# Sine and cosine of a spatial gate: theta by channels on full tiles, products carried to tokens by DMA transposes

## The chip, the cores and the metric

One core of a Trainium2 chip runs the whole program in one launch. The metric is the device time of one execution in microseconds. TensorE (PE) does the matrix products, VectorE (DVE), ScalarE (ACT) and GpSimd (POOL) the elementwise work, SyncE (SP) issues all DMAs.

## What is computed

Three layers in a row, for 4 batches of 576 tokens and 512 channels: an attention (8 heads, half of them local, half strided), a gated layer, and the layer that the change is about. Cut to the latter, with `x` the output of the gated layer:

```python
def _moe2_ref(x, w_theta, w_tok_r, w_tok_i, w_ch):      # x: (4, 576, 512)
    theta = x @ w_theta
    cos_t, sin_t = (np.cos(theta), np.sin(theta))
    zr = x * cos_t
    zi = x * sin_t
    yr = np.einsum('ts,bsd->btd', w_tok_r, zr)           # mixes tokens
    yi = np.einsum('ts,bsd->btd', w_tok_i, zi)
    u = x + yr + yi
    return (u + np.maximum(u @ w_ch, 0.0)).astype(np.float32)
```

The kernel keeps every operand as two float16 numbers, a high part and the rest (a low part), and forms a product in three passes: high by high, low by high, high by low.

## The kernel before

The batches run one after the other, b = 0 to 3. Each has these stages on PE, named by the tile that the products go to:

- `v` (`main_v`), tokens on partitions: 48 matmuls of 512 columns, and 12 on the last 64 tokens; a layer norm on DVE and ACT turns it into `vn`.
- `u` and `sp` (`main_mid`): the two halves of the gate, channels on partitions, pairs of 288 columns.
- `x` (tiles `x20` to `x23`, four chunks of 128 channels): the gated layer's output. `x2_evac` (L622) copies it to `x2f` (float32), splits it into `x2h` (high and low), and issues two DMA transposes per chunk, high and low, each 128 x 640, that put the same numbers token-major into `zz`, a view of `zf`.
- `th` (L651 on): theta with tokens on partitions. Two pairs of full tiles of 128 tokens and one tile of the last 64, in `TH_ORDER` (0, 2, 1): 48 matmuls of 512 columns and 12 for the last 64 tokens, whose halves go to two halves of the array and are added by `fold_tail`. For each of the five token tiles (`ta`), on 512 channels: ACT rounds theta / 2 pi to an integer; DVE takes it off (`ta<-ta,th`) and clamps the rest (`ta<-ta`); ACT makes the absolute value, the cosine and the sine; POOL puts `x` together again from the transposed halves (`xt<-zf`); DVE multiplies twice (`ta<-ta,xt`); and each product is split into high (DVE or ACT) and low (DVE or POOL, `zf<-ta,zf`).
- `y` (`main_end`): the token mixing. `zz` has 9 slots of 128 rows (4 of cosine, 4 of sine, one with the last 64 tokens of both); each chunk of 128 channels takes 54 matmuls of 288 columns, that is 9 slots, 3 passes, 2 halves. Every chunk needs every slot. `TOK_GROUPS` lets chunks 0 and 1 start on slots 0 and 4 before the rest is there.
- `c`: the last product, and the output.

Around these run two things that have no stage of their own. `conv` turns the weights, which lie in memory as 64-bit floats, into float16 pairs (`tok_part` for the token weights), in batch 0. The attention of batch b + 1 runs in steps beside the stages of batch b (`sc`: scores; `sm`: softmax on DVE, ACT and POOL; `pT`: the transposed weights; `av`: the product with the values, which goes to `xT`, the input of `v`). When a step is written into the program is decided by a clock that counts PE columns: the stages are generators, and at every `yield` `others()` emits what is due.

After `main_mid(b)`, `drain(b + 1)` finishes the next batch's attention and `main_v(b + 1)` comes before `main_end(b)`; in batch 0 four steps of `main_end` (all of chunks 0 and 1) come ahead of that. So between `th` and `y` of one batch stands `v` of the next, but for the last batch, where `y` follows `th` directly.

All PE stages share three PSUM tiles `pm`; a stage waits until the tile three back is read. Each engine and each queue works in the order of its own list; a scheduler in the language makes the lists from the program, with the work of `hv`, `ha` and `hg` put ahead of other work.

Of the kernel before, what the change touches and what calls it, by code (L numbers as in the profile page):

```python
# [27 lines left out]
PI_IN = 3.1415925  # L28
# [39 lines left out]
def kernel(  # L68
# [175 lines left out]
    def tok_part(r, i):  # L244
        o = r * NF + i
        w = (w_tr, w_ti)[r]
        prep_w(wtok[:, 0, o, :], wtok[:, 1, o, :], w[i * P:(i + 1) * P, :], S)

    def tok_tail():
# [338 lines left out]
    def main_mid(b):  # L588
# [59 lines left out]

        for pr in TH_ORDER:
            rows = P if pr < 2 else TL  # L650
            nt = 2 if pr < 2 else 1  # L651
# [244 lines left out]
```

## Time and profile before

| what | us |
|---|---|
| median of 3 runs (557.25 to 558.96) | 557.27 |
| the profiled execution | 559.4 |
| its span, first to last instruction | 557.6 |
| PE busy in it | 488.9 |
| DVE busy in it | 402.2 |
| ACT busy in it | 314.8 |
| POOL busy in it | 178.0 |
| mean granted clock of TensorE | 0.969 of 2.4 GHz |

The busy time of an engine is what its instructions cover. The profile also gives, for each idle stretch of an engine, what ended it: `[2.60 <-POOL zf L110]` in the timeline says that the engine stood for 2.60 us until an instruction of POOL that writes `zf` was done. Line 110 is the helper through which all work of `hv`, `ha` and `hg` goes, L492 the matmul of a stage, L420, L389 and L456 the attention's. The granted clock of a stretch is 1.00 at 2.4 GHz and 0.50 at 1.2 GHz.

### The profile page before, as it was taken

To read this page: it belongs to the slowest core of one execution; us is meant where nothing else is said; L and a number is where in the kernel's file an instruction comes from. 1 tells how busy PE (TensorE), PEld (TensorE's weight loads), DVE (VectorE), ACT (ScalarE), POOL (GpSimd) and SP (SyncE) were. 2 spreads that over 40 slices of the span, in tenths; PEclk is the share of its full clock that TensorE was granted. 3 is DMA by queue.
4 is the path that set the end of the run, shared out by engine and by line. 5 is a ranking of instruction groups with operands and counts; after the bars stand their busy time and mean duration, and the time that the engine had idled before them with its cause. 6 is when DMAs were issued, how large, how long until landed. Compare 5 with 4: busy or idle time off the path is not lost. (4 is left out here: it accounts for less than half of the span.)

```text
span 557.6 us, 10326 instructions
## 1 busy us (share of the span) xinstructions
PE 488.9 (88%) x3836; PEld 346.6 (62%) x3836; DVE 402.2 (72%) x998; ACT 314.8 (56%) x767; POOL 178.0 (32%) x131
## 2 busy tenths in 40 slices
PE   5888969596788969998997979999989999998896
PEld 4664747474355647776644767777437777764575
DVE  2787889989999989889489958874499531228712
ACT  3776868576776467776457267765563212145401
POOL 0464245566564540002062320010252500106320
PEclk9889989989989998999999998999999999999899
DMA  7666665548125214875810016523400010050002
GB/s 277 198 228 242 210 213 190 162 121 177 36 73 165 69 40 95 214 165 136 170 21 0 1 30 160 153 39 65 69 0 1 1 59 29 1 95 2 1 0 86
DMA packets 59478, 55.69 MB, mean 100 GB/s; under 512 B 43554, under 2 KB 44578, under 8 KB 59428
## 3 DMA queue, kind: packets, MB, share of 16 engines
q1 hardware_dynamic: 59428, 55.04, 36.3%
q8 instruction: 30, 0.49, 0.4%
q14 instruction: 20, 0.16, 0.1%
HBM read 40.08 MB, written 4.72 MB: 80 GB/s over the span
## 5 line engine op out<-in xcount | busy, mean ns | idle before, releaser
L492 PE MATMUL y<-wtok,zf 128*128 128x288 f16 x864 | 111.3, 289 | 13.2 <-POOL zf L110 4.9
L492 PEld LDWEIGHTS <-zf 128*128 128x128 f16 x864 | 84.0, 99 | 40.1 <-POOL zf L110 6.0
L338 ACT ACTIVATE sm<-sm,st 96x128 f32<-96x128 f32 (+1 forms) x132 | 51.4, 391 | 14.5 <-DVE st L329 13.1
L492 PE MATMUL sp<-wsp,vn 128*128 128x288 f16 x384 | 51.6, 289 | 2.0 <-ACT vn L110 1.9
L492 PE MATMUL c<-x2h,wch 128*128 128x288 f16 x384 | 51.7, 296 | 0.7 <-ACT o L110 0.7
L492 PE MATMUL th<-wth,x2h 128*128 128x512 f16 (+1 forms) x240 | 52.0, 394 | 0.0
L492 PE MATMUL x<-zf,wout 128*128 128x288 f16 x384 | 51.1, 292 | 0.0
L110 POOL TENSOR_TENSOR x2h<-x2f,x2h 128x576 f16<-128x576 f32 x20 | 27.9, 1396 | 71.0 <-issue 37.6
L492 PE MATMUL u<-xT,win 128*128 128x288 f16 x384 | 49.3, 286 | 0.0
L492 PEld LDWEIGHTS <-vn 128*128 128x128 f16 x416 | 40.6, 99 | 13.0 <-ACT vn L110 2.2
L110 POOL TENSOR_TENSOR zf<-u,zf 128x576 f16<-128x576 f32 x8 | 11.1, 1392 | 114.9 <-ACT zf L110 114.9
L110 POOL TENSOR_TENSOR xt<-zf 128x512 f32<-128x512 f16 (+1 forms) x20 | 32.2, 1616 | 47.0 <-DMA zf<-x2h 24.4
L492 PEld LDWEIGHTS <-wch 128*128 128x128 f16 x384 | 38.5, 101 | 11.7 <-issue 0.9
L492 PEld LDWEIGHTS <-wout 128*128 128x128 f16 x384 | 37.6, 100 | 10.5 <-issue 0.4
L553 PE MATMUL v<-win,xT 128*128 128x512 f16 x192 | 43.8, 379 | 0.3 <-ACT xT L357 0.3
L492 PEld LDWEIGHTS <-win 128*128 128x128 f16 x384 | 37.3, 98 | 9.2
L492 PEld LDWEIGHTS <-x2h 128*128 128x128 f16 (+1 forms) x240 | 21.7, 103 | 26.3 <-issue 5.8
L329 DVE CUSTOM_DVE_ANT_0 sm<-sc,mask 96x128 f32<-96x128 f32 (+1 forms) x132 | 32.1, 280 | 3.4 <-PE av L420 2.0
L110 ACT ACTIVATE ta<-ta 128x512 f32<-128x512 f32 (+1 forms) x40 | 23.9, 618 | 17.9 <-DVE ta L110 17.8
L553 PEld LDWEIGHTS <-xT 128*128 128x128 f16 x192 | 18.6, 98 | 21.6 <-ACT xT L357 0.6
L110 POOL TENSOR_TENSOR zf<-ta,zf 128x512 f16<-128x512 f32 x16 | 23.3, 1456 | 18.8 <-ACT zf L110 18.8
L110 DVE TENSOR_TENSOR ta<-ta,xt 128x512 f32<-128x512 f32 x32 | 25.7, 836 | 3.9 <-ACT ta L110 3.9
(127 smaller groups left out, 941.8 us busy)
## 6 DMA issues: line engine op xcount, KB each, us to landing
qs<-in_qd_dram SPq DMA_DIRECT2D x16, 288.0 KB, 3.0
out_dram<-o SPq DMA_DIRECT2D x15, 288.0 KB, 2.6
x2f<-in_w_in_dram SPq DMA_DIRECT2D x8, 512.0 KB, 5.5
ks<-in_kl_dram SPq DMA_DIRECT2D x8, 304.0 KB, 3.2
k<-in_kzs_dram SPq DMA_DIRECT2D x4, 576.0 KB, 5.4
wstg<-in_w_tr_dram SPq DMA_DIRECT2D x4, 576.0 KB, 4.6
wstg<-in_w_ti_dram SPq DMA_DIRECT2D x4, 576.0 KB, 3.9
ks<-in_ks_dram SPq DMA_DIRECT2D x8, 288.0 KB, 3.5
```

The source lines that it names most:

```text
L110: return f(*args, **kwargs)
L329: nc.vector.tensor_tensor_reduce(out=sm[0:R, n, :], in0=sc[n][0:R], in1=mask[0:R, mi, :], op0=ALU.add, op1=ALU.min, scale=-0.125, scalar=3e38,
L338: nc.scalar.activation(sm[0:R, n, :], sm[0:R, n, :], AF.Exp, bias=st[0:R, 1, n:n + 1], scale=-1.0, accum_out=st[0:R, 2, n:n + 1])
L492: nc.tensor.matmul(ps, lhs, rhs, **kw)
L553: nc.tensor.matmul(ps, xh[:, xe, c, i * P:(i + 1) * P], win[:, we, c, DM:2 * DM], start=(c == 0 and n == 0), stop=(c == NC - 1 and n == 2))
```

## The change

Theta is computed with channels on partitions, like the stages around it. `th_mm` uses the weights as the stationary operand: four chunks of 128 channels, 24 matmuls of 288 columns each, no tile of 64 rows. `z_chunk` then works on 128 channels by 576 tokens: ACT rounds theta, now as a number of turns, to an integer; DVE forms the fraction in one step from PSUM (`TURNS` is the factor); the clamp is gone, since the sine is taken of `TURN`, a little under 2 pi, times the fraction; ACT makes absolute value, cosine and sine; DVE multiplies both halves by `x2f` in one instruction of 128 x 1152; `split` makes the high part on ACT and the low part on DVE, each 128 x 1152, into one of two buffers `zbs` that lie in `vn`. Two DMA transposes of 128 x 1152 per chunk carry them token-major into `zz`, nine blocks each: columns 0 to 575 of a buffer are cosine, 576 to 1151 sine, so the slots of `zz`, and with them the rows of `wtok`, run on without a gap. The transposes of `x2h`, the sums `xt`, and the padding of `x2h` fall away.

`main_end` takes the chunks one by one over all nine slots; a chunk needs only its own 128 channels of `zz`. Its first four steps in batch 0 no longer come ahead of `main_v(1)`.

```diff
-            for e in range(2):
-                nc.sync.dma_start_transpose(out=zz[:, 0:NF + 1, e, m * P:(m + 1) * P], in_=x2h[:, e, m, :])
...
-            for t in range(nt):
-                a = s2("ta")
...
-                ha.activation(ia, tv, AF.Copy, scale=1.0 / (PS * 2 * math.pi))
-                hv.scalar_tensor_tensor(bv, ia, -2 * math.pi * PS, tv, op0=ALU.mult, op1=ALU.add)
-                hv.tensor_scalar(bv, bv, PI_IN * PS, -PI_IN * PS, op0=ALU.min, op1=ALU.max)
-                ha.activation(av, bv, AF.Abs)
-                ha.activation(av, av, AF.Sin, bias=halfpi[r], scale=-1.0 / PS)
-                ha.activation(bv, bv, AF.Sin, scale=1.0 / PS)
-                o = 2 * pr + t
-                H[E_XADD[b > 0]].tensor_tensor(xv, zz[r, o, 0, :], zz[r, o, 1, :], ALU.add)
...
+        def z_chunk(m, ps):
+            a = s2(f"ta{m}")
+            flat = a.rearrange("p a n -> p (a n)")
+            turns, f = a.bitcast(I32)[:, 0, :], a[:, 1, :]
+            ha.activation(fold(turns), halves(ps), AF.Copy, scale=TURNS)
+            hv.scalar_tensor_tensor(fold(f), halves(ps), TURNS, fold(turns), op0=ALU.mult, op1=ALU.subtract)
+            ha.activation(a[:, 0, :], f, AF.Abs)
+            ha.activation(a[:, 0, :], a[:, 0, :], AF.Sin, bias=halfpi, scale=-TURN)
+            ha.activation(f, f, AF.Sin, scale=TURN)
+            hv.tensor_tensor(a, a, x2f[:, m, :].unsqueeze(1).broadcast_to([P, 2, S]), ALU.mult)
+            zb = zbs[m % 2]
+            split((zb[:, 0, :], zb[:, 1, :]), flat, H[E_ZLO[m + 4 * (b > 0)]])
+            for e in range(2):
+                nc.sync.dma_start_transpose(out=zz[:, :, e, m * P:(m + 1) * P], in_=zb[:, e, :])
...
+        for m in range(NC):
             ps = pm(f"y{m}")
-            tok_mm(ps, m, (0, 1, 4, 5, 2, 3, 6, 7, 8), True, True)
-            tok_evac(m, ps)
-            yield
+            for i in range(NZ):
+                for n, (ze, we) in enumerate(PASS):
+                    mm2(ps, zz[:, i, ze, m * P:(m + 1) * P], wtok[:, we, i, :],
+                        i == 0 and n == 0, i == NZ - 1 and n == 2)
+                if i == NZ - 1:
+                    tok_evac(m, ps)
+                if i % 3 == 2:
+                    yield
...
         if b + 1 < B:
-            for _ in range(4 if b == 0 else 0):
-                next(end, None)
-                others()
             drain(b + 1)
             run_main(main_v(b + 1))
```

The lists of the engines change with it. On DVE in the last batch, from its first instruction on `th`, before:

```order
L110 SCALAR_TENSOR_TENSOR ta_5568<-ta_5568,th0_5543 128x512
L110 TENSOR_SCALAR ta_5568<-ta_5568 128x512
L110 SCALAR_TENSOR_TENSOR ta_5583<-ta_5583,th0_5543 128x512
L110 TENSOR_SCALAR ta_5583<-ta_5583 128x512
L110 TENSOR_TENSOR ta_5568<-ta_5568,xt_5569 128x512 x2
L110 CAST zf_95<-ta_5568 128x512
L110 TENSOR_TENSOR zt_5611<-th2_5598,xt_5613 64x512
L110 TENSOR_TENSOR zf_95<-ta_5568,zf_95 128x512
L110 TENSOR_TENSOR ta_5583<-ta_5583,xt_5584 128x512 x2
L110 CAST zf_95<-ta_5583 128x512
L110 SCALAR_TENSOR_TENSOR ta_5612<-ta_5612,zt_5611 64x512
L110 TENSOR_TENSOR zf_95<-ta_5583,zf_95 128x512
```

These are two of the five token tiles and the start of the third; the list goes on in the same way for 14 more rows. The whole of this work in the same batch, now:

```order
L108 SCALAR_TENSOR_TENSOR ta0_5569<-th0_5525,ta0_5569 128x576
L108 SCALAR_TENSOR_TENSOR ta1_5586<-th1_5526,ta1_5586 128x576
L108 TENSOR_TENSOR ta0_5569<-ta0_5569,x2f_96 128x1152
L108 SCALAR_TENSOR_TENSOR ta2_5622<-th2_5597,ta2_5622 128x576
L108 TENSOR_TENSOR vn_94<-ta0_5569,vn_94 128x1152
L108 TENSOR_TENSOR ta1_5586<-ta1_5586,x2f_96 128x1152
L108 SCALAR_TENSOR_TENSOR ta3_5658<-th3_5633,ta3_5658 128x576
L108 TENSOR_TENSOR ta2_5622<-ta2_5622,x2f_96 128x1152
L108 TENSOR_TENSOR vn_94<-ta1_5586,vn_94 128x1152
L108 TENSOR_TENSOR vn_94<-ta2_5622,vn_94 128x1152
L108 TENSOR_TENSOR ta3_5658<-ta3_5658,x2f_96 128x1152
L108 TENSOR_TENSOR vn_94<-ta3_5658,vn_94 128x1152
```

Thirty instructions on DVE have become twelve, and none of them has 64 rows or reads what POOL wrote.

On ACT in batch 0, at the end of the next batch's attention (`pT32` is its last transposed softmax, `xT1_93` its output, the input of `v`), before:

```order
L110 ACTIVATE zf_95<-ta_1563 128x512
L421 ACTIVATE pT32_1464<-av_1536 128x512
L121 ACTIVATE kT_1838<-ks_1881 128x608
L121 ACTIVATE qT_1941<-qs_1943 128x576
L110 ACTIVATE ta_1592<-ta_1592 64x512
L110 ACTIVATE ta_1654<-th1_1607 128x512
L110 ACTIVATE ta_1592<-ta_1592,halfpi_76 64x512
L110 ACTIVATE ta_1592<-ta_1592 64x512
L110 ACTIVATE ta_1639<-ta_1639 128x512
L357 ACTIVATE xT1_93<-av_1617 128x18x14
```

and now:

```order
L108 ACTIVATE vn_94<-ta2_1611 128x1152
L108 ACTIVATE ta3_1654<-ta3_1654,halfpi_76 128x576
L108 ACTIVATE ta3_1654<-ta3_1654 128x576
L423 ACTIVATE pT32_1456<-av_1546 128x512
L119 ACTIVATE kT_1853<-ks_1904 128x608
L292 ACTIVATE vT_1910<-vs_1850 128x768
L108 ACTIVATE vn_94<-ta3_1654 128x1152
L359 ACTIVATE xT1_93<-av_1622 128x18x14
```

The attention's copy `pT32` stood in the middle of the sine work, after two of five tiles; it now stands behind the last sine of the last chunk, and the last `xT` behind the last high part.

On PE in batch 0, where `v` of batch 1 meets that (`sc_1952` is the first score of batch 2's attention), now:

```order
L494 MATMUL v2_1748<-win_78,xT1_93 64x512
L435 LDWEIGHTS qT_1852
L435 MATMUL sc_1952<-kT_1853,qT_1852 96x128
L435 LDWEIGHTS qT_1852
L435 MATMUL sc_1952<-kT_1853,qT_1852 96x128
L391 MATMUL av_1622<-pT32_1456,v32_1276 64x126 x4
L435 LDWEIGHTS qT_1852
L435 MATMUL sc_1952<-kT_1853,qT_1852 96x128
```

Before, the same `av` product (there `av_1617`) stood between matmuls of `y0` and `y1`. Those have moved behind `v`, and ahead of `av` now stand 21 of the 60 matmuls of `v`, the ones that don't need the last heads.

## Rows read from the trace of the kernel before

**Rows 1.** waits of TensorE: engine, line, releaser: us in total, times, longest us

```profile
PE sc L433 <- DVE st L329: 8.9, 6, 4.1
...
PE y L492 <- POOL zf L110: 4.9, 2, 2.6
...
PE y L492 <- ACT vr L110: 3.9, 4, 1.0
PE v L492 <- DVE ta L110: 3.6, 2, 1.9
```

**Rows 2.** timeline of TensorE, batch 3: start us, us, instructions [idle before <-releaser]

```profile
483.20 11.92 PE L492 MATMUL x<-zf,wout 128*128 128x288 f16 x96
494.96 12.04 PE L492 MATMUL th<-wth,x2h 128*128 128x512 f16 x60
506.84 1.34 PE L492 MATMUL y<-wtok,zf 128*128 128x288 f16 x8
510.78 5.01 PE L492 MATMUL y<-wtok,zf 128*128 128x288 f16 x38 [2.60 <-POOL zf L110]
517.82 1.03 PE L492 MATMUL y<-wtok,zf 128*128 128x288 f16 x7 [2.04 <-ACT zf L110]
519.35 21.80 PE L492 MATMUL y<-wtok,zf 128*128 128x288 f16 x163 [0.50 <-DVE zf L110]
```

**Rows 3.** timeline of TensorE, batch 1: v of batch 2, and a score inside c

```profile
284.14 10.52 PE L553 MATMUL v<-win,xT 128*128 128x512 f16 x48
...
333.76 0.61 PE L433 MATMUL sc<-kT,qT 128*96 128x128 f16 x8 [2.48 <-DVE st L329]
```

**Rows 4.** timeline of TensorE, batch 0: the end of y

```profile
208.05 0.61 PE L433 MATMUL sc<-kT,qT 128*96 128x128 f16 x8 [4.11 <-DVE st L329]
...
209.69 3.21 PE L492 MATMUL c<-x2h,wch 128*128 128x288 f16 x15
```

**Rows 5.** timeline of VectorE, batch 0: its first instruction on theta

```profile
148.09 0.67 DVE L110 SCALAR_TENSOR_TENSOR ta<-ta,th 128x512 f32<-128x512 int32 x1
```

**Rows 6.** stretches: us; busy us of PE, PEld, DVE, ACT, POOL; PEclk, DMA share, GB/s

```profile
157.60:209.60 52.00, 42.49 (x321) 28.09 (x319) 50.22 (x101) 30.71 (x59) 25.96 (x16) 0.99 0.28 80
```

**Rows 7.** groups by shape, all batches: busy us, mean ns of one, idle before

```profile
L110 DVE TENSOR_TENSOR ta<-ta,xt 128x512 f32<-128x512 f32 x32 | 25.7, 836 | 3.9 <-ACT ta L110 3.9
...
L110 ACT ACTIVATE ta<-ta 128x512 f32<-128x512 f32 x32 | 19.0, 617 | 0.1
...
L110 ACT ACTIVATE ta<-ta,halfpi 128x512 f32<-128x512 f32 x16 | 11.4, 715 | 0.2
...
L110 DVE SCALAR_TENSOR_TENSOR x2f<-y,x2f 128x576 f32<-128x576 f32 x16 | 12.1, 753 | 19.8 <-PE y L492 19.6
...
L110 ACT ACTIVATE x2f<-x 128x576 f32<-128x576 f32 x16 | 10.2, 646 | 12.8 <-PE x L492 12.7
...
L110 ACT ACTIVATE vn<-vr 128x1024 f16<-128x1024 f32 x8 | 8.1, 1043 | 0.2 <-DVE vr L110 0.2
...
L110 DVE TENSOR_TENSOR vn<-vr,vn 128x1024 f16<-128x1024 f32 x4 | 4.8, 1212 | 0.0
```

**Rows 8.** DMA issues by line: count, median us to landing

```profile
zf<-x2h SPq DMA_TRANSPOSE x32, 2.6
...
pT<-ph SPq DMA_TRANSPOSE x22, 3.1
```

**Rows 9.** instructions on zf from SyncE, all 32 transposes: landing

```profile
DMA to landing us min/median/max: 2.6/2.6/4.4
```

**Rows 10.** stretches as in rows 6: batch 3's eight transposes, then three after waits

```profile
486.00:508.00 22.00, 21.98 (x143) 12.95 (x140) 8.37 (x14) 12.05 (x20) 4.97 (x4) 1.00 0.35 61
111.00:116.00 5.00, 4.40 (x24) 2.90 (x25) 3.03 (x14) 3.42 (x12) 2.97 (x4) 0.50 0.09 14
334.00:338.00 4.00, 4.00 (x27) 2.76 (x25) 3.78 (x15) 3.48 (x16) 0.51 (x1) 0.63 0.30 80
518.00:524.00 6.00, 5.50 (x32) 3.61 (x31) 5.97 (x10) 3.55 (x7) 1.56 (x2) 0.72 0.00 0
```

More of the change, by code (lines that the diff above doesn't have):

```diff
@@ L27 @@
 SS = SPS * VNS
-PI_IN = 3.1415925
+TURN = 6.283185
+TURNS = 1.0 / (PS * 2 * math.pi)
 AHEAD = 200
@@ L153 @@
     zf = const.tile([P, (NF + 1) * 2 * DM + 2 * NC * S], F16, name="zf")
-    zz = zf[:, 0:(2 * NF + 1) * 2 * DM].rearrange("p (i e d) -> p i e d", i=2 * NF + 1, e=2)
+    zz = zf[:, 0:NZ * 2 * DM].rearrange("p (i e d) -> p i e d", i=NZ, e=2)
     gT = zf[:, (NF + 1) * 2 * DM:].rearrange("p (e c s) -> p e c s", e=2, c=NC)
+    zbs = [vn.rearrange("p i e d -> p (i e d)")[:, i * 4 * S:(i + 1) * 4 * S].rearrange("p (e n) -> p e n", e=2)
+           for i in range(2)]
     x2f = const.tile([P, NC, S], F32, name="x2f")
-    x2h = const.tile([P, 2, NC, (NF + 1) * P], F16, name="x2h")
+    x2h = const.tile([P, 2, NC, S], F16, name="x2h")
     def s2(name):
@@ L242, in sp_tail, with tok_part @@
                                        op0=ALU.mult, op1=ALU.subtract)
[L244 to L249, printed above, removed]
-        stg, x = stage()
-        for j, w in enumerate((w_tr, w_ti)):
-            nc.sync.dma_start(stg[j * TL:(j + 1) * TL, :], w[T0:S, :])
-        part(wtok[:, 0, 2 * NF, :], wtok[:, 1, 2 * NF, :], from_f64(stg, x, S), True)
+    def tok_part(i):
+        stg, x = stage()
+        r = 0
+        while r < P:
+            g = i * P + r
+            w, k = (w_tr, g) if g < S else (w_ti, g - S)
+            n = min(P - r, S - k)
+            nc.sync.dma_start(stg[r:r + n, 0:S], w[k:k + n, :])
+            r += n
+        part(wtok[:, 0, i, :], wtok[:, 1, i, :], from_f64(stg, x, S), True)
     SOFF = [0, 126, 252, 378, 448]
@@ new lines, in th_mm @@
+        def th_mm(m, ps, cs):
+            for c in cs:
+                for n, (we, xe) in enumerate(PASS):
+                    mm2(ps, wth[:, we, c, m * P:(m + 1) * P], x2h[:, xe, c, :],
+                        c == 0 and n == 0, c == NC - 1 and n == 2)
+        tiles = [pm(f"th{i}") for i in range(2)]
+        for cs in ((0, 1, 2), (3,)):
+            for m in range(2):
+                th_mm(m, tiles[m], cs)
+                if cs[0] == 3:
+                    z_chunk(m, tiles[m])
+                yield
@@ L692, in main_mid @@
+        for m in (2, 3):
+            ps = pm(f"th{m}")
+            th_mm(m, ps, range(NC))
+            z_chunk(m, ps)
             yield
     def main_end(b):
-        slot = list(range(NF)) + list(range(NF + 1, 2 * NF + 1)) + [NF]
-        def tok_mm(ps, m, tiles, first, last):
-            for i in tiles:
-                for n, (ze, we) in enumerate(PASS):
-                    mm2(ps, zz[:, slot[i], ze, m * P:(m + 1) * P], wtok[:, we, i, :],
-                        first and i == tiles[0] and n == 0, last and i == tiles[-1] and n == 2)
@@ L707, in tok_evac @@
             split((x2h[:, 0, m, 0:S], x2h[:, 1, m, 0:S]), x, H[E_YLO[m + 4 * (b > 0)]], E_YHI[m + 4 * (b > 0)])
-        tiles = [pm(f"y{i}") for i in range(2)]
-        for part, grp in enumerate(TOK_GROUPS):
-            end = part == len(TOK_GROUPS) - 1
-            for m in range(2):
-                tok_mm(tiles[m], m, grp, part == 0, end)
-                if end:
-                    tok_evac(m, tiles[m])
-                yield
-        for m in (2, 3):
-            ps = pm(f"y{m}")
-            tok_mm(ps, m, (0, 1, 4, 5, 2, 3, 6, 7, 8), True, True)
-            tok_evac(m, ps)
-            yield
+        for m in range(NC):
+            ps = pm(f"y{m}")
+            for i in range(NZ):
[6 more added lines that the diff above has]
+                    yield
         for m0 in (0, 2):
@@ L760 @@
     timed(list(sq_parts(wth, w_th)) + [switch], *CONV_TH)
-    timed([lambda r=r, i=i: tok_part(r, i) for i in range(NF) for r in range(2)] + [tok_tail], *CONV_TOK)
+    timed([lambda i=i: tok_part(i) for i in range(NZ)], *CONV_TOK)
     timed(sq_parts(wch, w_ch), *CONV_CH)
```

41 lines of the change are left out of this document (3 added, 38 removed).

## The prediction

> **What bounds the kernel now.** TensorE, stage by stage; so I read first what it waits for, then its timeline in each batch, then which engine is full there. Of the waits [rows 1], four kinds belong to the stretch from theta to the end of `y` and `c`: on POOL's and ACT's share of the products (`zf`), on ACT's `vr`, on DVE's `ta`, and on DVE's `st`, the scores of the attention that wait for the softmax before them. In batch 3 nothing stands between `th` and `y` [rows 2]: `y` starts at 506.84 on two of its nine slots, then waits 2.60, 2.04 and 0.50 us, 5.1 in all, for the rest of the products. In batches 1 and 2 `v` of the next batch lies between, and the products are not waited for; what is late there is a PSUM tile: the last part of `v` waits for a theta tile that DVE has not read, twice, 3.6 us together, and `y` four times for a tile that ACT has not emptied, 3.9 us [rows 1]. In batch 1 a score inside `c` then waits 2.48 us [rows 3], in batch 0 one at the end of `y` 4.11 us [rows 4]. Batch 0 is another regime: while it does theta and `y`, DVE is busy 50.2 of 52.0 us [rows 6], with weight conversion and two attentions beside the sines.
>
> **TensorE's own work.** Theta goes from 60 matmuls to 96 of 288 columns. `x` has the same shape: 96 from 483.20 to 494.96 [rows 2], 11.76 us, 0.1225 us each. `th` took 494.96 to 506.84, 11.88 us. Four batches give 0.5 us. `y` keeps its 216 matmuls.
>
> **Batches 1 and 2: the PSUM waits go.** Count from the start of `th`. The first chunk is complete after 42 matmuls (18 + 18 + 6), at 5.15 us; theta ends at 11.8, `v` at about 24, where `y` wants the tile that ACT empties with its first `vr`. On ACT's new list ahead of that `vr` stand four copies from PSUM at 0.65, eight absolute values and sines (0.617 for 512 columns, so 0.69 for 576), four cosines (0.715, so 0.80), and three high parts of 1152 (1.043 for 1024, so 1.17) [rows 7]: 2.6 + 5.5 + 3.2 + 3.5 = 14.8 us. From 5.15 that is 20.0, plus 1.0 for `vr` itself: 3 us to spare, of which a function table's load takes a part. Theta's PSUM tiles are now read by the first two instructions of a chunk's work, copy and subtraction (0.65 + 0.75 [rows 7]), where the last token tile stood at the end of a long list; each tile is wanted again 2 us or more after that. So 3.6 + 3.9 = **7.5 us** go, with nothing behind them that is late next. If ACT runs 3 us behind this count, the waits on `vr` come back: 3.6 is the low end.
>
> **Batch 1, the score inside c.** Its wait of 2.48 us [rows 3] is followed by a stretch of 4 us at a granted clock of 0.63 [rows 10], which costs 0.37 x 4 = 1.5. DVE gets to the scores late because `v`'s norm stands behind the last products. `y` now yields three times per chunk, so scores stand 36 matmuls (4.4 us) apart instead of 54, 54 and 11. But the softmax behind each score is as long as it was. Between 0 and 4.0 I take **2.5 us**.
>
> **Batch 3: one wait for three.** Here the new chain is bare. From 5.15 us: copy 0.65, subtraction 0.75, absolute value 0.69, cosine 0.80, sine 0.69 give 8.75. The multiply of 1152 is 2.25 times one of 512, which takes 0.84 on average [rows 7] with POOL busy beside it; POOL has nothing to do now, so I take 1.4: 10.2. ACT does chunk 1's pieces meanwhile and comes to the high part at about 10.9, done 12.1; the low part (1.21 for 1024, so 1.36 [rows 7]) is done at 13.5. Then the transposes. One of 5 blocks lands in 2.6 us, one of 8 in 3.1 [rows 8]; for 9 I take 3.3, with 4.4, the slowest of the 32 [rows 9], times 9/5 = 7.9 as the far end. The second pass of `y0` needs the low part: 16.8, where TensorE was free at 11.8. So a wait of 5.0 us stands where 5.1 stood. Chunks 1 to 3 have 6.6 us of `y` before them each, and ACT and DVE need under 4 per chunk, so they are hidden. The clock was 0.72 in the 6 us after the old waits [rows 10], 1.7 us lost; I expect the same. Together **0**, from -3 to +3.
>
> The rows say how fast these transposes run: eight of 164 KB keep the DMA engines 0.35 of 22 us busy [rows 10], 0.96 us each, 170 GB/s; for 295 KB that makes 1.7 us, a pair per chunk 3.5 of a chunk's 4, which still fits. The Trainium skill (DMA: Bandwidth & Descriptors, Latency and other measured facts) gives 261 GB/s for such a transpose; by that one would take an estimated 1.1 us, land 0.6 sooner, and the sum below would be 0.6 us larger. This trace is slower than the page.
>
> **Batch 0: a cover is given up, VectorE is relieved.** DVE's first instruction on theta comes at 148.09 [rows 5] because conversions stand ahead of it; they still do. Thirty DVE instructions become twelve: 4 x (0.75 + 1.4 + 1.36) = 14 us. But the attention's last steps, on which `v` hangs, now stand behind the last sine on ACT. After 148.8 ACT has left: four absolute values and four sines 5.5, cosines 3.2, two copies 1.3, three high parts 3.5, and some 2.5 of other work: 164.8. Then the attention's copy, key and value splits, the last high part and `xT` on ACT and DVE, about 4.1: 168.9. TensorE has by then done theta and 21 matmuls of `v` and stands for ten us or more. The other 39 at 0.22 (10.52 for 48 [rows 3]) end at 177.4, `y` (216 x 0.1225 = 26.5) at 203.9, three scores and one `av` between them at 0.6 make 206.3. Before, `c` began at 209.69 [rows 4]. That is 3.4 us, less what the clock costs after so long a stand: 5 us at 0.50 in one stretch after a wait [rows 10] are 2.5 us. Between 0.9 and 3.4 I take **2 us**; from -5 to +10.
>
> That a stand costs clock is also a rule of the Trainium skill (TensorE: Matmul & The Clock Gate, HAM oscillation): each idle stretch that is long enough starts the next burst at half speed. It speaks against this change, which joins short waits into one in batch 3 and one in batch 0. By the row after batch 3's old waits the loss there is 1.7, by that of the long wait 2.5; the sum would be 0.8 us smaller by the second. The three stretches shown agree with the rule.
>
> **Sum.** 0.5 + 7.5 + 2.5 + 0 + 2 = 12.5 us of the profiled 559.4, which lies 0.4% over the median. So 557.27 x (1 - 12.5 / 559.4) = 544.8.
>
> **Rivals.** (a) VectorE was what held batch 0, not the attention's tail: with eighteen of its instructions and POOL's sums beside them gone, conversions finish earlier too, and the stand before `v` shrinks to what it was. For it: 50.2 of 52 us busy. Against: the list on ACT. Then 8 us more, 537. (b) The tail in batch 0 costs more than counted, since a chunk's third high part also waits for the first chunk's transposes to give its buffer free, and ACT stands with the attention's copy behind it; with 5 us lost there and the scores in `c` as before, 9.5 us go: 554. (c) The transposes land late. Place: the hop from `zbs` to `zz`. Each us over 3.3 costs 1 us in batch 3 and, through the reused buffers and ACT's list, 1 to 2 in batch 0; in batches 1 and 2 nothing up to about 8 us, then up to 1 each. From 8 us (the far end above is 7.9) the gain of 12.5 is gone, and at 9 it is 559.5 or more, slower than before. For it: no row shows nine blocks, and eight follow each other in 12 us. Against: 5 blocks and 8 blocks differ by 0.5 us. (d) The change doesn't do what it says: waits for `vr` come back in batches 1 and 2 as they were, and batch 0 loses 4: 557.
>
> **How the numbers follow.** The forecast, 539 to 550, 0.57; (a) 530 to 539, 0.15; (b) 550 to 555, 0.17; (d) within 0.3% of 557.3 (about what a measurement of this kernel can tell from no change), 0.04; (c) 0.07. Leaving out (c), (d) and the ends of (a) and (b) gives a range from 533 to 554. Faster 0.89, same 0.04, slower 0.07.
>
> **What would show it.** Right: no `vr` or `ta` among the waits of `v` and `y` in batches 1 and 2; in batch 3 a single wait of 4 to 6 us before `y0`, ended by a transpose; in batch 0 a stand of about ten us before or inside `v`, and no long wait in `y`; landing of 3 to 3.6 us. Wrong: waits inside `y` on transposes of chunks 1 to 3, DVE still full in batch 0, or the score waits in `c` unchanged.

## The result and the profile after

The changed kernel takes 544.5 us (median; 543.5 to 544.8), the kernel before 558.1 beside it: a ratio of 0.975, 95% interval 0.971 to 0.978. One of the changed kernel's four executions took 2742.9 us and is left out of these figures; no trace of it was kept. The forecast was 544.8, in a range from 533 to 554. The profiled execution took 544.3 us with a span of 542.2, where before had 557.6; the mean granted clock is 0.972 (0.969).

To see where the 15.4 us of span went, cut each profile where `u` of a batch starts. Batch 0 then includes theta and `y` of batch 0 with `v` of batch 1 between them, and so on; the last column ends with the span. The kernels further down are in the same table.

| kernel | to first u | batch 0 | batch 1 | batch 2 | batch 3 | span |
|---|---|---|---|---|---|---|
| before | 59.9 | 165.9 | 122.4 | 109.5 | 99.9 | 557.6 |
| after | 60.5 | 165.0 | 113.1 | 105.4 | 98.2 | 542.2 |
| after, once more (E12) | 59.2 | 165.5 | 113.6 | 105.4 | 98.2 | 542.0 |
| E1 one gap per chunk | 59.9 | 164.3 | 114.1 | 105.4 | 98.2 | 541.9 |
| E2 before, y by chunks | 59.5 | 170.8 | 119.9 | 112.6 | 99.8 | 562.5 |
| E3 transposes twice | 59.4 | 175.1 | 120.9 | 105.4 | 104.3 | 565.1 |
| E4 early y | 60.3 | 161.3 | 115.5 | 105.4 | 97.9 | 540.4 |
| E5 low parts of batch 0 on POOL | 60.0 | 169.4 | 112.9 | 105.4 | 99.0 | 546.7 |
| E6 before, angle alone | 59.5 | 165.7 | 116.3 | 109.9 | 98.3 | 549.6 |
| E7 w_ch early | 60.7 | 162.4 | 113.2 | 105.4 | 99.1 | 540.8 |
| E7 w_ch late | 59.3 | 167.1 | 116.0 | 105.4 | 97.9 | 545.7 |
| E9 low parts twice, batches 1, 2 | 61.2 | 165.7 | 117.2 | 105.4 | 98.2 | 547.7 |
| E10 order of batch 3 | 60.7 | 164.4 | 115.0 | 105.4 | 93.7 | 539.1 |
| E11 E4, E7 early and E10 | 60.1 | 164.6 | 113.1 | 105.4 | 93.7 | 537.0 |

Batch 1 gave 9.3 us, batch 2 4.1, batch 3 1.7, batch 0 1.0; the start lost 0.6. Batch 1 of E10, which no edit touches, differs from that of after by 1.9, and that of E7 late, whose edit lies in batch 0, by 2.9; batch 0 of after, E12, E9 and E10, which have the same program there, lies between 164.4 and 165.7. So a difference under 3 us in batch 1, or under 1.5 in batch 0, says nothing by itself. Batch 2 repeats within 0.1.

What TensorE waits for now, the rows that answer to [rows 1] (engine, line, releaser: us, times, longest):

```profile
PE av L422 <- DVE xT L360: 8.4, 5, 2.9
...
PE sc L435 <- DVE st L331: 4.4, 2, 4.0
PE y L494 <- DMA zf<-vn: 4.1, 2, 3.2
PE av L391 <- ACT pT L423: 3.4, 1, 3.4
```

No `vr` and no `ta` is left among the releasers of `v` and `y`, and POOL's and ACT's `zf` have given way to a transpose. Scores wait 4.4 us for `st` instead of 8.9. The timeline of TensorE in batch 1, answering to [rows 3], has no wait in `v` or `y`, and the score inside `c` waits 0.39 where it waited 2.48:

```profile
282.72 10.52 PE L555 MATMUL v<-win,xT 128*128 128x512 f16 x48
293.17 1.49 PE L494 MATMUL v<-win,xT 128*64 128x512 f16 x12
294.59 13.40 PE L494 MATMUL y<-wtok,zf 128*128 128x288 f16 x108
...
328.70 0.61 PE L435 MATMUL sc<-kT,qT 128*96 128x128 f16 x8 [0.39 <-DVE st L331]
```

VectorE is busy 366.5 us (402.2), POOL 119.3 (178.0). What takes the place of the multiplies and low parts in [rows 7], by shape (busy us, mean ns of one, idle before):

```profile
L108 DVE TENSOR_TENSOR vn<-ta,vn 128x1152 f16<-128x1152 f32 x16 | 22.3, 1396 | 6.5 <-ACT vn L108 6.5
L108 DVE TENSOR_TENSOR ta<-ta,x2f 128x1152 f32<-128x1152 f32 x16 | 21.6, 1351 | 8.1 <-ACT ta L108 8.1
```

The forecast had 1.36 us for the first and 1.4 for the second. Batch 3, answering to [rows 2]: two waits on transposes, 4.14 us together, in place of 5.14:

```profile
481.21 11.92 PE L494 MATMUL th<-x2h,wth 128*128 128x288 f16 x96
496.36 0.42 PE L494 MATMUL y<-wtok,zf 128*128 128x288 f16 x2 [3.22 <-DMA zf<-vn]
497.70 28.06 PE L494 MATMUL y<-wtok,zf 128*128 128x288 f16 x214 [0.92 <-DMA zf<-vn]
```

Batch 0, answering to [rows 4]: `v` of batch 1 stands 4.3 us for the attention's tail, and a score in `y` still waits four:

```profile
164.02 1.11 PE L391 MATMUL av<-pT,v 128*64 128x126 f32 x8 [3.37 <-ACT pT L423]
...
166.31 0.69 PE L435 MATMUL sc<-kT,qT 128*96 128x128 f16 x5 [0.91 <-DVE kT L287]
...
176.75 17.81 PE L494 MATMUL y<-wtok,zf 128*128 128x288 f16 x144
...
203.40 0.61 PE L435 MATMUL sc<-kT,qT 128*96 128x128 f16 x8 [3.98 <-DVE st L331]
...
210.88 1.39 PE L494 MATMUL c<-x2h,wch 128*128 128x288 f16 x10
```

### The profile page after: what moved, and what is told of

It reads as the page before. It is cut to its first block, busy times and chain, and to the rows that moved or that the text cites. A ratio compares the mean times of both kernels' runs of the same rounds, so it can differ in the third digit from the quotient of the medians.

```text
span 542.2 us, 10436 instructions
## 1 busy us (share of the span) xinstructions
PE 485.4 (90%) x3980; PEld 361.3 (67%) x3980; DVE 366.5 (68%) x926; ACT 310.8 (57%) x743; POOL 119.3 (22%) x94
## 5 line engine op out<-in xcount | busy, mean ns | idle before, releaser
L494 PEld LDWEIGHTS <-zf 128*128 128x128 f16 x864 | 85.4, 100 | 28.7 <-DMA zf<-vn 4.8
L340 ACT ACTIVATE sm<-sm,st 96x128 f32<-96x128 f32 (+1 forms) x132 | 51.3, 390 | 13.9 <-DVE st L331 13.6
L494 PE MATMUL x<-zf,wout 128*128 128x288 f16 x384 | 52.5, 297 | 0.0
L108 POOL TENSOR_TENSOR x2h<-x2f,x2h 128x576 f16<-128x576 f32 x20 | 26.3, 1316 | 113.3 <-DVE x2h L108 50.4
L494 PE MATMUL c<-x2h,wch 128*128 128x288 f16 x384 | 48.8, 286 | 2.3 <-ACT o L108 2.3
L494 PE MATMUL th<-x2h,wth 128*128 128x288 f16 x384 | 48.4, 286 | 0.0
L494 PEld LDWEIGHTS <-wth 128*128 128x128 f16 x384 | 37.4, 98 | 9.5 <-issue 0.2
L108 ACT ACTIVATE x2h<-x2f 128x576 f16<-128x576 f32 x24 | 16.2, 681 | 30.5 <-DVE x2f L108 30.2
L108 DVE SCALAR_TENSOR_TENSOR x2f<-y,x2f 128x576 f32<-128x576 f32 x16 | 12.0, 752 | 28.8 <-PE y L494 28.7
L108 ACT ACTIVATE o<-c 128x576 f32<-128x576 f32 (+1 forms) x17 | 10.3, 613 | 30.3 <-PE c L494 30.0
L108 DVE TENSOR_TENSOR ta<-ta,x2f 128x1152 f32<-128x1152 f32 x16 | 21.6, 1351 | 8.1 <-ACT ta L108 8.1
```

Of the source, the lines that this page charges most:

```text
L108: return f(*args, **kwargs)
L340: nc.scalar.activation(sm[0:R, n, :], sm[0:R, n, :], AF.Exp, bias=st[0:R, 1, n:n + 1], scale=-1.0, accum_out=st[0:R, 2, n:n + 1])
L494: nc.tensor.matmul(ps, lhs, rhs, **kw)
```

## The experiments

Two theories stood after the two traces. One: the change pays because VectorE and ScalarE have fewer and larger steps, so that PSUM tiles and softmaxes are in time. The other: it pays because `y` now has three gaps per chunk for other work, so that scores no longer crowd into `c`. Open beside that were the price of the transposes and what holds batch 0.

### E1, one gap per chunk of y

```diff
-                if i % 3 == 2:
+                if i == NZ - 1:
                     yield
```

> The changed kernel, with one gap for other work per chunk of y (at its end) in place of three; nothing else differs. Between before and after, batch 1 gained 9.3 us, of which 3.2 before y, 1.9 in y, 3.2 in c. Theory A: y and c gained because the attention's scores stand 36 matmuls apart in y, so that no softmax is late in c. Then batch 1 loses 3 to 5 us of this, a wait of 2 us or more for DVE's st stands in c or at the end of y again, and the whole takes 547.5 to 550. Theory B (rival): y and c gained because VectorE has eighteen instructions fewer and comes to the softmax in time, wherever the gaps stand. Then 544 to 546, and the score in c still waits under 0.6 us.

Measured: 541.7 us, ratio 0.967 [0.961, 0.973]. Batch 1 changed by 1.0 us, less than two profiles differ by; no score in its `c` waits at all, and `c` with all that lies in it took 14.1 us against 15.2. So the gaps are not what made the gain: theory B.

### E2, the kernel before with the new order of y alone

```diff
-        for part, grp in enumerate(TOK_GROUPS):
...
+        for m in range(NC):
+            ps = pm(f"y{m}")
+            for k, i in enumerate((0, 1, 4, 5, 2, 3, 6, 7, 8)):
...
+                if k % 3 == 2:
+                    yield
...
-            for _ in range(4 if b == 0 else 0):
+            for _ in range(6 if b == 0 else 0):
```

> The kernel before with only y's order changed: chunk by chunk over all nine slots, three gaps for other work per chunk; six early steps in batch 0 instead of four, so that y0 and y1 lie ahead of v as before. Theta, sines and products stay token-major. Theory A (the gaps in y give the gain in batch 1's y and c): 3 to 5 us less in batch 1, 1.3 more in batch 3, where y0 can no longer run on its first slots together with y1: 553 to 556. Theory B (VectorE's relief gives it): 557 to 559.5, and the score in c waits 2 us or more as before. Under both, the waits for vr and ta in batches 1 and 2 stay, 7.5 us together.

Measured: 564.0, ratio 1.009 [1.006, 1.012]: slower by 0.9%, outside both expectations. Its waits name the reason:

```profile
PE y L492 <- DVE zf L110: 13.7, 11, 2.1
```

`y0` goes through all nine slots at once, and the last token tiles are not there: 13.7 us on VectorE's products, where the same view of before has 9.1 on products in all (POOL 4.9 [rows 1], VectorE 2.2, ACT 2.0). Batch 0 lost 4.9 us, batch 2 3.1. In batch 1 `c` fell from 18.4 to 15.4 us, so the gaps do help a score that is late; E1 shows that nothing is late any more once VectorE is relieved. The order chunk by chunk is no gain of its own, it is made possible by products that are complete chunk by chunk.

### E6, the angle alone in the kernel before

```diff
-                hv.scalar_tensor_tensor(bv, ia, -2 * math.pi * PS, tv, op0=ALU.mult, op1=ALU.add)
-                hv.tensor_scalar(bv, bv, PI_IN * PS, -PI_IN * PS, op0=ALU.min, op1=ALU.max)
...
+                hv.scalar_tensor_tensor(bv, tv, TURNS, ia, op0=ALU.mult, op1=ALU.subtract)
...
```

> The kernel before with only the angle changed: a fraction of turns, the clamp gone (on VectorE, one instruction of 128 x 512 fewer for each of four token tiles and one of 64 rows, about 0.5 us each). All else is token-major as before. Theory A (VectorE's list is what stands behind the late PSUM tiles and scores in batches 1 and 2): these waits shrink by about 1 us per batch, 1 to 3 us less in all, and nothing in batch 3 but 0.5: 555 to 557.5. Theory B (rival): the angle alone is worth nothing, since the waits hang on POOL's sums, on tails of 64 rows and on ACT's order: 558 to 559.5.

Measured: 553.6, ratio 0.991 [0.988, 0.995], more than expected. Five VectorE instructions fewer per batch were worth 6.1 us in batch 1, 1.6 in batch 3, and nothing in batch 2. TensorE's timeline in batches 1 and 2 says why:

```profile
296.17 1.63 PE L493 MATMUL y<-wtok,zf 128*128 128x288 f16 x12 [2.15 <-ACT vr L111]
298.86 11.92 PE L493 MATMUL y<-wtok,zf 128*128 128x288 f16 x96 [1.07 <-ACT vr L111]
...
411.00 2.09 PE L493 MATMUL y<-wtok,zf 128*128 128x288 f16 x12 [2.19 <-ACT vr L111]
413.70 25.98 PE L493 MATMUL y<-wtok,zf 128*128 128x288 f16 x204 [0.61 <-ACT vr L111]
```

The waits of `v` for `ta`, 3.6 us [rows 1], are gone from these batches, but 2.1 of them came back as longer waits of `y` for `vr` (6.0 us in all, 3.9 before [rows 1]), and the next 12 matmuls in batch 2 took 2.09 us instead of 1.63: VectorE's lateness hid ScalarE's. In batch 2, where no score is late, the waits of `v` and `y` fell only from 3.69 to 2.80 us, and the clock took that back. It is the third figure from the end in this stretch of E6 (columns as in [rows 6]); in before it is 1.00 in the same place, from 418 to 424 us:

```profile
411.00:417.00 6.00, 5.38 (x33) 3.64 (x33) 6.00 (x12) 2.13 (x3) 1.15 (x1) 0.72 0.01 3
```

Only the channel-major form took both waits away, 4.1 us in batch 2. In batch 1 the earlier VectorE was also worth 2.7 in `c`. So a third to a half of the whole gain is the angle's (4.4 of 13.6 us by the medians, 8.0 of 15.4 by the profiles, where E6's execution took 551.5 us), the rest the layout's.

### E9, half of VectorE's relief given back in batches 1 and 2

```diff
+            if b in (1, 2):
+                hv.tensor_tensor(zb[:, 1, :], flat, zb[:, 0, :], ALU.subtract)
             for e in range(2):
```

> The changed kernel, with the low part of each chunk's products made twice on VectorE in batches 1 and 2 (the same values to the same place): 8 instructions of 1.35 us more, 5.4 us in each of the two batches, which gives VectorE back about half of the instruction time that the change took off it there; the transposes of these batches leave 1.35 us later. Theory A: batch 1's gain in y and c (5.2 us) is VectorE's relief; then most of what is given back shows there: batch 1 grows by 2.5 to 5.5 us with waits for DVE's st in y or c, batch 2 by 0 to 1: 545.5 to 550 against 541.5 to 544.5 for the changed kernel. Theory B (rival): the relief is not what counts, since VectorE has room in both batches; the gain came from the shorter chain (norm of v behind fewer, larger steps): under 1.5 us more in all.

Measured: 547.9, ratio 0.979 [0.973, 0.986]; batch 1 grew by 4.1 us against after (3.6 against E12), batch 2 by nothing. In `y` and `c` of batch 1 the scores wait again:

```profile
317.40 0.61 PE L435 MATMUL sc<-kT,qT 128*96 128x128 f16 x8 [1.43 <-DVE st L331]
...
323.03 0.61 PE L435 MATMUL sc<-kT,qT 128*96 128x128 f16 x8 [0.61 <-DVE st L331]
...
334.12 0.61 PE L435 MATMUL sc<-kT,qT 128*96 128x128 f16 x8 [0.33 <-DVE st L331]
```

`y` took 31.1 us, gaps included, against 28.8 in after, E10 and E12. Of the 4.1, 2.4 lie there; another 1.7 lie in `x`, ahead of the added work, and belong to the spread that E10 has too. The interval of the whole time overlaps that of after, so it is the timeline that decides. That is theory A at its low end: about half of the relief is worth 2.4 us in batch 1 and 0 in batch 2. VectorE's busy time from theta to the next `u` of batch 1 is 59.2 us before, 49.1 after and 53.4 here (the third figure behind the stretch's length, in this order):

```profile
272.00:348.00 76.00, 68.57 (x519) 45.78 (x517) 59.24 (x149) 42.71 (x96) 22.35 (x15) 0.98 0.22 52
271.00:338.00 67.00, 65.68 (x549) 48.27 (x548) 49.11 (x121) 41.13 (x88) 8.96 (x6) 1.00 0.39 80
274.00:344.00 70.00, 66.56 (x555) 48.70 (x553) 53.42 (x127) 41.80 (x89) 8.40 (x6) 1.00 0.35 76
```

### E3, each transpose of the products twice

```diff
-            for e in range(2):
+            for e in (0, 0, 1, 1):
                 nc.sync.dma_start_transpose(out=zz[:, :, e, m * P:(m + 1) * P], in_=zb[:, e, :])
```

> The changed kernel, with each transpose of the products issued twice in a row, the same data to the same place. A pair then becomes four: the last landing of a chunk comes some 2.6 us later (two more issues of 1.3 us on SyncE's queue; by the 1.7 us that 295 KB take, 3.4). Theory A: this is paid once in batch 3, before y0 (its wait of 4.1 grows to 6.7 to 7.5), once or twice in batch 0, and not in batches 1 and 2, where v lies between: 549 to 553. Theory B (rival): the DMA engines are full (four times 1.7 = 6.8 us per chunk, more than the 4 between chunks), so chunks 1 to 3 are waited for as well, and the attention's transposes queue behind them in batches 1 and 2: 555 or more. Theory C: the transposes are hidden in batch 0 as well, and only batch 3 pays: 547 to 548.5.

Measured: 567.9, ratio 1.016 [1.011, 1.021]: theory B, and the whole gain of the change lost. Each transpose still lands after 3.4 us; they queue. Stretches of this kernel, then of after, with the transposes of batches 0 and 1 in them (columns as in [rows 6]):

```profile
155.00:182.00 27.00, 22.10 (x123) 11.41 (x122) 13.85 (x16) 13.24 (x19) 1.79 (x1) 0.87 1.02 185
293.00:320.00 27.00, 27.00 (x193) 17.70 (x192) 18.86 (x39) 11.57 (x16) 0.00 (x0) 1.00 0.98 175
```

```profile
156.00:171.00 15.00, 10.65 (x49) 4.36 (x48) 14.29 (x23) 14.68 (x28) 1.80 (x1) 0.77 0.87 170
284.00:299.00 15.00, 15.00 (x91) 8.15 (x90) 13.78 (x19) 11.10 (x15) 0.00 (x0) 1.00 0.92 147
```

Sixteen transposes fill the DMA engines for 27 us; eight already take 0.87 to 0.92 of them for 15. The first group below is VectorE's timeline in batch 0, the second TensorE's in batches 0 and 3:

```profile
182.69 0.43 DVE L201 TENSOR_SCALAR wx<-wstg 128x512 int32<-128x512 int32 x1 [8.46 <-DMA wstg<-in_w_ch_dram]
```

```profile
211.10 1.01 PE L435 MATMUL sc<-kT,qT 128*96 128x128 f16 x8 [13.50 <-DVE st L331]
...
516.53 0.66 PE L494 MATMUL y<-wtok,zf 128*128 128x288 f16 x2 [6.55 <-DMA zf<-vn]
520.11 28.55 PE L494 MATMUL y<-wtok,zf 128*128 128x288 f16 x214 [2.92 <-DMA zf<-vn]
```

In batch 3 the waits grew from 4.1 to 9.5. In batch 0 the loads of `w_ch` stand behind the transposes on SyncE's queue (the first leaves at 178.2 us, in after at 172.8); VectorE waits 8.5 us for them, and a score behind that work 13.5. In batch 1 VectorE's low parts wait 6.2 us for a buffer that is still being read, with the softmaxes behind them, and a score waits 5.1. In batch 2, with no score in `y`, all of it is hidden.

### E4, y0 and y1 of batch 0 ahead of v again

```diff
+            for _ in range(6 if b == 0 else 0):
+                next(end, None)
+                others()
             drain(b + 1)
```

> The changed kernel, with y0 and y1 of batch 0 ahead of v of batch 1 again (six steps of the new y, as the four steps of before were). Theory A: the cover that the change gave up is worth what TensorE stands before and in v of batch 1, 5 us, less what y0 waits for the first chunk's transposes: 539.5 to 543. Theory B (rival): VectorE and ScalarE set the end of batch 0 (sines, conversions, the attention's softmax), so TensorE stands somewhere else for as long, at y0 or later in y: 543.5 to 546. Theory C: v, and with it the norm that VectorE makes for the next u, comes 13 us later and TensorE then waits for that: 546 or more.

Measured: 542.3, ratio 0.970 [0.965, 0.974], not told apart from after (0.975 [0.971, 0.978] and, in E12, 0.974 [0.970, 0.977]). Batch 0 is 3.7 us shorter; batch 1 is 2.4 longer, within its spread. TensorE in batch 0:

```profile
160.31 0.42 PE L494 MATMUL y<-wtok,zf 128*128 128x288 f16 x2 [3.52 <-DMA zf<-vn]
161.68 5.14 PE L494 MATMUL y<-wtok,zf 128*128 128x288 f16 x29 [0.94 <-DMA zf<-vn]
...
204.16 0.61 PE L435 MATMUL sc<-kT,qT 128*96 128x128 f16 x8 [3.63 <-DVE st L331]
```

The time is at the slow end of theory A, the waits are theory B's: the stand of 4.3 us in `v` became one of 4.5 before `y0`, and the score in `y` waits as before. What batch 0 gained is mostly clock: from 156 to 176 us its mean is 0.92 here and 0.83 in after, an estimated 1.7 us of the twenty, and from 204 to 212 it is 1.00 here and 0.79 in after, another 1.7. The second part need not be the edit's, for E12 has 1.00 behind that wait without it. The cover that the change gave up was worth little as a cover, because the new `y` must itself wait for the transposes.

### E7, the conversion of w_ch 14 us earlier, or 8 later

```diff
-CONV_CH = (87.0, 14.1, 2.4)
+CONV_CH = (73.0, 14.1, 2.4)
```

> The changed kernel, with the conversion of w_ch (four parts on SyncE, ACT, VectorE and POOL) due 14 us earlier on the planned clock, so that it lies beside theta instead of v. In the changed kernel a part of it stands on VectorE at 197.8 to 202.4 of batch 0, ahead of the softmax for which a score in y waits 3.98 us. Theory A: this wait goes, and the stand before v grows by less than it: batch 0 gets 1 to 3.5 us shorter, 540 to 543. Theory B (rival): the conversion then stands among the sines, which end later, and v waits longer for the attention's copy behind them: batch 0 gets 1 to 6 us longer, 543.5 to 550.

The other kernel has 95.0 in the same place.

> The changed kernel, with the conversion of w_ch due 8 us later on the planned clock, after v's norm and not between its parts. Theory A (the conversion ahead of the softmax makes the score in y of batch 0 wait 3.98 us): the wait moves or goes; if the parts now stand behind that softmax, batch 0 gets 2 to 4 us shorter, 539 to 542. Theory B (rival): VectorE has the same work before c in any order, and the last part of w_ch, which c needs, comes later: c waits instead, 542 to 546. Theory C: the wait came from VectorE's norm of v, not from the conversion: no change, 541.5 to 544.5.

Measured: early 543.1, 0.972 [0.967, 0.977]; late 546.9, 0.979 [0.974, 0.985]. The first two rows are TensorE's in batch 0 with the early conversion, the third with the late one:

```profile
162.84 1.09 PE L422 MATMUL av<-ident,sm 128*128 128x128 f32 x4 [5.24 <-DVE xT L360]
...
195.10 0.61 PE L435 MATMUL sc<-kT,qT 128*96 128x128 f16 x8 [0.95 <-DVE st L331]
```

```profile
204.43 1.01 PE L435 MATMUL sc<-kT,qT 128*96 128x128 f16 x8 [5.48 <-DVE st L331]
```

Early, the score's wait of 3.98 falls to 0.95 and batch 0 is 2.6 us shorter, as theory A said, though in `v` 5.24 and 0.69 us are stood where it was 4.3. Late, the wait grows to 5.5 instead of going, batch 0 is 2.1 us longer, and the time lies above all three expectations: the conversion, begun later, still stands ahead of that softmax, until 203.5 us. Both fit the reading that this conversion, ahead of the softmax on VectorE, makes the score wait; for the whole time neither interval is clear of after's. In after, the start of that conversion and the softmax behind it on VectorE:

```profile
197.75 2.35 DVE L201 TENSOR_SCALAR wx<-wstg 128x512 int32<-128x512 int32 x1
...
202.42 0.28 DVE L331 CUSTOM_DVE_ANT_0 sm<-sc,mask 96x128 f32<-96x128 f32 x1
```

### E5, the low parts of batch 0 on POOL

```diff
-E_ZLO = 'vvvvvvvv'
+E_ZLO = 'ggggvvvv'
```

> The changed kernel, with the low parts of the products of batch 0 (four instructions of 128 x 1152) on POOL in place of VectorE; batches 1 to 3 as they are. Theory A: batch 0 is held by VectorE's list (conversions, norm of v, softmax), so 5.4 us less on it shorten batch 0 by 1 to 4 us, above all the wait of 3.98 us for DVE's st at the end of y: 540 to 543.5. Theory B (rival): batch 0 is held by ScalarE's list up to v and by the order on VectorE behind it, not by its sum; POOL takes 1.28 us for 576 columns where VectorE takes 0.75, so the low parts, the transposes and the buffers behind them come later: batch 0 the same or up to 4 us longer, 544 to 549.

Measured: 550.0, ratio 0.984 [0.979, 0.989]; batch 0 is 4.4 us longer. Both waits of TensorE in batch 0 grew:

```profile
165.51 1.11 PE L391 MATMUL av<-pT,v 128*64 128x126 f32 x8 [5.65 <-ACT pT L423]
...
207.05 1.01 PE L435 MATMUL sc<-kT,qT 128*96 128x128 f16 x8 [5.67 <-DVE st L331]
```

The waits are 2.3 us longer at the attention's `pT` and 1.7 at the score. The time is theory B's, a little above its end, but the experiment does not decide between the two, for VectorE was not relieved. The four low parts left its list, 6.1 us, but three of its four multiplies in batch 0, each beside a low part on POOL, took 3.05 us, where the fourth and all sixteen of after took 1.35. VectorE's busy time over the span fell by 1.0 us only, from 366.5 to 365.5. ScalarE's high parts wait for these multiplies, and the copy to `pT` stands behind them. One such pair, VectorE's timeline and then POOL's:

```profile
155.24 3.06 DVE L108 TENSOR_TENSOR ta<-ta,x2f 128x1152 f32<-128x1152 f32 x1 [1.37 <-ACT ta L108]
```

```profile
154.71 2.38 POOL L108 TENSOR_TENSOR vn<-ta,vn 128x1152 f16<-128x1152 f32 x1 [5.20 <-ACT vn L108]
```

### E10, the order of batch 3

```diff
+        runs = ((0, (0, 1, 2)), (1, (0,)), (0, (3,)), (1, (1, 2, 3))) if b == B - 1 else \
+            ((0, (0, 1, 2)), (1, (0, 1, 2)), (0, (3,)), (1, (3,)))
+        for m, cs in runs:
...
+            if b == B - 1 and m == 0:
+                for n, (ze, we) in enumerate(((0, 0), (0, 1), (1, 0))):
+                    for i in range(NZ):
```

> The changed kernel with two orders changed in batch 3 alone: theta's first chunk is complete after 30 matmuls in place of 42, and y0 uses the high parts of all nine slots with both weights before any low part. Theory A (the chain copy, sines, product, high part, transpose stands bare before y0, and each us off it counts in full): 12 matmuls are 1.47 us, so the first wait of y0 goes from 3.22 to 1.2 to 1.8, the second, 0.92, goes away; batch 3 gets 2 to 3 us shorter: 541 to 542. Theory B (rival): the fourth chunk of x2h comes too late for theta's first chunk, or ACT is the bound of the whole batch: the wait moves into theta or to y1: under 1 us, 543 to 544.5.

Measured: 540.9, ratio 0.965 [0.960, 0.969]. Batch 3 is 4.5 us shorter, more than theory A had. TensorE's timeline, then a stretch of this kernel and one of after, both from the first matmul of `y` (the clock is the third figure from the end):

```profile
482.69 11.92 PE L494 MATMUL th<-x2h,wth 128*128 128x288 f16 x96
496.10 26.63 PE L494 MATMUL y<-wtok,zf 128*128 128x288 f16 x216 [1.49 <-DMA zf<-vn]
```

```profile
496.00:504.00 8.00, 7.90 (x65) 6.33 (x66) 7.20 (x7) 6.68 (x9) 0.00 (x0) 1.00 0.64 122
```

```profile
496.00:504.00 8.00, 6.72 (x40) 4.60 (x41) 6.19 (x6) 5.04 (x6) 0.00 (x0) 0.79 0.88 167
```

The waits fell by 2.65 us, as expected: 1.73 in the first, and the second is gone. The other 1.9 is the clock: `y` runs at 26.63 us for 216 matmuls, where after took 28.48 without its waits. After a stand of 1.49 us the granted clock stays at 1.00, which is 2.4 GHz; after 3.22 and 0.92 it was 0.79 over 8 us, between the two levels. Other profiles bear this out: the eight with the order of after, which all wait 3.2 us first, take 29.1 to 30.3 us from the first to the last matmul of this `y`, and E11, which waits 1.48 us, takes 26.63 like E10. The Trainium skill (TensorE: Matmul & The Clock Gate, HAM oscillation) says that a stand which is long enough makes the next burst start at half speed; the two rows of E10 and after agree.

### E11, three edits together, and E12, after once more

E11 joins the diffs of E4, E7 early and E10. E12 is the changed kernel as it is.

> The changed kernel with three edits together: the order of batch 3 (theta's first chunk after 30 matmuls, low parts of y0 last), y0 and y1 of batch 0 ahead of v again, and the conversion of w_ch due 14 us earlier. Alone, by their spans per batch against the changed kernel's: 4.5 us in batch 3; 3.7 in batch 0, of which batch 1 gave back 2.4; 2.6 in batch 0. Theory A (they act in different places and add): 4.5 + 1.3 + 2.6 = 8.4 us less than the changed kernel in the same call: 535 to 538. Theory B (rival): the two in batch 0 fill the same stand, before and in v, so only one counts: 4.5 + 2 = 6.5 less or smaller: 538 to 541.

> The changed kernel itself, once more, beside the three edits together. It shows by how much the spans of the batches differ between two profiles of one program: batch 2 by under 0.2 us, as the experiments that don't touch it had it; batches 0 and 1 by 1 to 2 us, if the differences seen there without an edit in the place (x of batch 1 took 14.8 or 16.5 us before theta) come from the run. Time: 541 to 545.

Measured: E11 539.3, ratio 0.966 [0.963, 0.969]; E12 543.7, 0.974 [0.970, 0.977]. Beside one another on one chip the three edits gain 0.8%, the intervals apart. By the spans that is 5.0 us, and 4.5 of them are batch 3's. TensorE in batch 0 of E11:

```profile
158.87 0.66 PE L494 MATMUL y<-wtok,zf 128*128 128x288 f16 x2 [6.32 <-DMA zf<-vn]
...
204.57 1.01 PE L435 MATMUL sc<-kT,qT 128*96 128x128 f16 x8 [3.56 <-DVE st L331]
```

The two edits of batch 0 do not add: with the early conversion theta ends 4.3 us sooner than in E4 (152.43 against 156.68), but the first transposes have landed only 1.4 us sooner (158.87 against 160.31), and `y0`, now early, waits 6.32 us for them. Together they leave batch 0 where it was: theory B, in its stronger form. E10's edit alone gave the same ratio and is the version to keep.

## Why the prediction was right, point by point

The time was right to 0.3 us, and that close it is luck. The forecast gain of 12.5 us stands against 15.4 by the spans and 13.6 by the medians taken beside one another: the scores of batch 1 and batch 3 gave 3.4 us more than written, batch 0 1.0 less, and the forecast started from a median of 557.3 that was 558.1 beside the changed kernel.

**TensorE's own work.** Right: the 96 theta matmuls take 11.92 us, as those of `x` did [rows 2], 0.12 less than before per batch.

**PSUM waits in batches 1 and 2, 7.5 us.** Right. Batch 2, which holds nothing else, gave 4.1, for 3.75 of waits and 0.12 of theta. The count of ScalarE's list holds too: its first `vr` in batch 2 ends 20.9 us after theta's start at 382.11 (21.0 written), ahead of `y` at 405.74:

```profile
401.99 1.00 ACT L108 ACTIVATE vr<-v 128x1024 f32<-128x1024 f32 x1
```

E6 adds what the prediction did not say: these are two engines' lateness, one behind the other, and taking VectorE's away alone took only 0.9 us off the waits of batch 2 and nothing off its time.

**The score inside c of batch 1, 2.5 us.** Under-sized. `c` gave 3.2, close to the far end of 4.0, and the scores in `y`, not counted, about 1 more. The reason given for the gain, scores spaced wider by the new gaps, was the wrong one for this kernel: E1 takes the gaps away and loses nothing, E9 gives VectorE work back and loses 2.4. Only where VectorE is still late, in E2, do the gaps help `c`. "The softmax behind each score is as long as it was" overlooked that it starts earlier.

**Batch 3, 0 us.** The chain was right step by step: the multiply starts 8.9 us after theta (8.75 written), `y0`'s second pass at 16.5 (16.8), landing 3.2 to 3.3 (3.3). The wait was 4.1, in two parts, for 5.0 in one, and 1.7 us came back. The cost of the clock was written as 1.7 us and E10 shows 1.9.

**Batch 0, 2 us.** The step that failed. `v` came on time: `xT` at 168.6 (168.9 written), `y` at 176.75 (177.4). TensorE stood 4.3 us there, not ten: theta itself began 5.7 us later than before (138.59, 132.87), behind more of the attention (36 of the matmuls of L422 ahead of it, where before had 28 of the same at L420) and its waits. But "no long wait in y" was wrong: a score waits 3.98 us at 203.40, because the conversion of `w_ch` now stands on VectorE ahead of its softmax, at 197.8 to 202.4; E7 moves that wait in both directions. `c` begins at 210.88, and in E12 at 208.26, where before had 209.69 and the forecast 206.3. The batch is 1.0 shorter, in E12 0.4, which is within its spread: of the 2 us nothing is shown.

**The rivals.** (a), VectorE as the bound of batch 0, falls with the result: VectorE is busy 8.8 us less from the first `u` to the next (155.1 before, 146.3 now), and the batch hardly shorter. E5 can't decide it. (c), late transposes, did not happen (median landing 3.3 us, the longest 5.6). But E3, which doubles the traffic as well, suggests that its price was too low in batch 1: it cost 5.4 us of waits in batch 3, 10.1 in batch 0 and 7.8 in batch 1, where (c) had 1 us for 1, 1 to 2, and nothing up to 8. What was overlooked is who stands behind: SyncE's queue holds weight loads, and VectorE's low part, waiting for a buffer, holds the softmaxes. The time of (d) doesn't follow from its words: 3.9 us of waits and 6 of batch 0 on top of the forecast are 554.7, not 557.

**Open.** Batch 0 got shorter by an early `y` (E4, 3.7 us) or by an early conversion (E7, 2.6 us), but not by both together (E11), and in the whole time neither is told apart from after; what sets its length was not found. How much of VectorE's relief comes from fewer instructions and how much from POOL standing idle beside them (22.4 us busy from theta to the next `u` of batch 1 before, 9.0 after) was not separated; E5 shows that POOL's work can lengthen VectorE's.

## What to carry to other kernels

When an engine off the bound is late, look at what stands behind its late step and at the next engine that is late in its shadow: in batch 2 relieving one of two took 0.9 us off 3.7 of waits and gained nothing, relieving both gained 4.1. A layout that completes its results in the order in which they are used makes an order of work possible that costs time without it. And a wait of TensorE at the end of a bare chain (one with no other work beside it) can be dearer than its length: 2.65 us off the waits of batch 3 were worth 4.5, since the clock no longer fell behind them. And work that is moved from a busy engine to an idle one can lengthen what the busy one does beside it (E5).

## What the runs showed of the hardware

Eight DMA transposes of 128 x 1152 (2 bytes), close behind one another, keep the DMA engines 0.87 to 0.92 busy for 15 us at 147 to 170 GB/s, and sixteen 0.98 to 1.02 for 27 at 175 to 185 (batch 0's rows hold some weight loads too): in these stretches the kernel has little or no DMA time left, though its mean is 41%. The landing of each does not show it, 3.3 us in after and 3.4 with twice as many; the queue does. The Trainium skill (DMA: Bandwidth & Descriptors, Latency and other measured facts) gives 261 GB/s for a DMA transpose whose middle dimension isn't contiguous, as here; these rows stay under it with the engines full. A VectorE multiply of 128 x 1152 took 3.05 us beside POOL's low parts and 1.35 without them (E5). And the clock after like waits is not always the same: batch 0 of after waits 3.98 us, of E12 3.86, and the next 8 us, first of after, then of E12, ran at 0.79 and at 1.00.

```profile
204.00:212.00 8.00, 8.00 (x67) 5.68 (x65) 6.74 (x20) 5.31 (x17) 1.68 (x2) 0.79 0.28 64
```

```profile
203.00:211.00 8.00, 8.00 (x81) 6.33 (x78) 6.71 (x20) 5.37 (x17) 1.74 (x2) 1.00 0.38 57
```
